# Attention and a normalised MLP on one core: the inverse deviation moved from GpSimd to two ScalarE activations, and the row made by one GpSimd instruction

## The chip, the cores and the metric

The kernel runs on one core of one Trainium2 chip. The metric is the device time of one execution in microseconds. The four executions of the kernel before lie between 312.97 and 314.12 us (0.4%), so differences of one percent are visible here. TensorE (PE) does the matrix products, VectorE (DVE) and ScalarE (ACT) do elementwise work and empty PSUM (the memory that matrix products are written to), GpSimd (POOL) casts and normalises rows, and SyncE (SP) issues transfers.

## The reference, cut to what matters

Eight batches of causal attention with a window of 64 (8 heads, 576 positions, head size 64) give rows `x` of 512 values. Each row is normalised and goes through a two-layer network with a residual:

```python
mu = np.mean(x, axis=-1, keepdims=True)
var = np.mean((x - mu) ** 2, axis=-1, keepdims=True)
xn = (x - mu) / np.sqrt(var + 1e-06) * g_ln
ch = np.maximum(xn @ w_ch1, 0.0) @ w_ch2
return x + ch
```

The change concerns `(x - mu) / sqrt(var + 1e-06)` alone. The kernel folds `g_ln` into the first weight matrix.

## The kernel before

The rows are handled in nine groups of 512 (the last holds the tails of all batches), and each group in four blocks of 128 rows. While TensorE runs the network of group g, the other engines prepare the rows of group g + 1. For groups 2 to 8 the row `z` of a block is made by four GpSimd instructions, from the mean and variance that VectorE left in `mvg`:

```python
def z_step(g, kb):
    z = p_blk.tile([128, DM], FP16, tag="z", ...)
    xv = x_norm[(g, kb // 2)][:, kb % 2, :]
    mu, var = mvg[g][:, kb, 0:1], mvg[g][:, kb, 1:2]
    # ... groups 0 and 1 go another way
    nc.gpsimd.tensor_scalar(out=ve, in0=var, scalar1=1.0, scalar2=EPS, op0=ALU.mult, op1=ALU.add)
    nc.gpsimd.tensor_tensor(out=rs, in0=ve, in1=mhalf, op=ALU.pow)
    nc.gpsimd.tensor_scalar(out=nm, in0=mu, scalar1=rs, scalar2=-1.0, op0=ALU.mult, op1=ALU.mult)
    nc.gpsimd.tensor_scalar(out=z, in0=xv, scalar1=rs, scalar2=nm, op0=ALU.mult, op1=ALU.add)
```

The first layer of a group is 16 units. Each fills one 128x512 PSUM tile with four matmuls, and ScalarE empties it with a Relu. There are only two such tiles (`bufs=2`), so TensorE can be at most two units ahead of ScalarE:

```python
ps_mm = ctx.enter_context(tc.tile_pool(name="psmm", bufs=2, space=PSUM))
def l1(hc):
    hps = ps_mm.tile([128, 512], FP32, tag="mm", ...)
    for kc in range(NKC):
        nc.tensor.matmul(out=hps, lhsT=w1g[:, kc, ...], rhs=zT[g][:, kc, :], ...)
    nc.scalar.activation(out=hrT[:, hc, :], in_=hps, func=AF.Relu, bias=0.0, scale=1.0)
```

The second layer is emptied by VectorE. Work for the next group is hung into numbered places after these units: `at(i, f, ...)` calls `f` after unit i. The built program keeps the written order for each engine, and the traces show ScalarE working through its instructions in that order, so a place decides what an instruction stands in front of.

The softmax here doesn't subtract the row's maximum and nothing guards it: scores larger than these inputs give would overflow.

Of the kernel before, what the change touches and what calls it, by code (L numbers as in the profile page):

```python
# [10 lines left out]
FP32 = mybir.dt.float32  # L11
# [3 lines left out]
AF = mybir.ActivationFunctionType  # L15
ALU = mybir.AluOpType
# [4 lines left out]
def kernel(  # L21
# [10 lines left out]
    nc = tc.nc  # L32
# [4 lines left out]
    NGRP = B + 1  # L37
# [3 lines left out]
    EPS = 1e-6  # L41
    XQ = 3
    XZ = 2
    scale = 1.0 / (D ** 0.5)
# [19 lines left out]
    mbias = p_const.tile([128, 64], FP16, tag="mbias", name="mbias")  # L64
    magt = p_const.tile([128, 4], FP32, tag="magt", name="magt")
    gT = p_const.tile([128, NKC], FP32, tag="gT", name="gT")
    mhalf = p_const.tile([128, 1], FP32, tag="mhalf", name="mhalf")
    w1g = p_const.tile([128, NKC, HID], FP16, tag="w1g", name="w1g")
    w2s = p_const.tile([128, NHC, DM], FP16, tag="w2s", name="w2s")
    w2v = w2s[:, :, :].rearrange("p (c e) (f d) -> p c e f d", e=2, f=2)  # L70
# [228 lines left out]
    def b_step(g, kb):  # L299
# [29 lines left out]
        if g < 2:  # L329
            z_step(g, kb)  # L330

    def z_step(g, kb):
        z = p_blk.tile([128, DM], FP16, tag="z", name=f"z_{g}_{kb}")
        zsd[(g, kb)] = z
        xv = x_norm[(g, kb // 2)][:, kb % 2, :]
        mu, var = mvg[g][:, kb, 0:1], mvg[g][:, kb, 1:2]
        if g < 2:
            nc.vector.tensor_scalar(out=z, in0=xv, scalar1=mu, scalar2=None, op0=ALU.subtract)
            return
        t = p_blk.tile([128, 3], FP32, tag="rsz", name=f"rsz_{g}_{kb}")  # L340
        ve, rs, nm = (t[:, i:i + 1] for i in range(3))
        nc.gpsimd.tensor_scalar(out=ve, in0=var, scalar1=1.0, scalar2=EPS, op0=ALU.mult, op1=ALU.add)  # L342
        nc.gpsimd.tensor_tensor(out=rs, in0=ve, in1=mhalf, op=ALU.pow)
        nc.gpsimd.tensor_scalar(out=nm, in0=mu, scalar1=rs, scalar2=-1.0, op0=ALU.mult, op1=ALU.mult)
        nc.gpsimd.tensor_scalar(out=z, in0=xv, scalar1=rs, scalar2=nm, op0=ALU.mult, op1=ALU.add)  # L345

    def zt_step(g, kb, eng="act"):
        z = zsd.pop((g, kb))
# [225 lines left out]
    nc.vector.memset(mask, 1.0)  # L574
    nc.vector.memset(magt, RSQRT_MAGIC)
    nc.vector.memset(ones1, 1.0)
    nc.vector.memset(mhalf, -0.5)
    nc.gpsimd.affine_select(
        out=mask[0:64], in_=mask[0:64], compare_op=ALU.is_gt, fill=0.0,
        base=0, channel_multiplier=1, pattern=[[-1, 64]],  # L580
# [85 lines left out]
    for g in range(NGRP):  # L666
        units, s_sums = mlp_units(g, (8, 16)[g] if g < 2 else 0, g == 0, g > 1)
        slots = [[] for _ in range(len(units) + 1)]

        def at(i, f, *a):  # L670
            slots[min(i, len(slots) - 1)].append((f, a))

        b = g + 1
        if g == 0:
            at(0, b_step, 0, 3)
            at(1, zt_step, 0, 2)
            at(3, zt_step, 0, 3)
            at(4, newton, 0, 0, 4)
            at(11, t_main, 1, 0, 0, 1)
            at(12, t_main, 1, 1, 0, 1)  # L680
            at(13, vB_cur, 1, 0, 1)
            at(13, vB_prev, 1, 0, 1)
            at(13, vB_cur, 1, 1, 1)
            at(13, vB_prev, 1, 1, 1)
            at(16, s_mm, 1, 0)
            at(16, s_mask, 1, 0)
            at(17, s_mm, 1, 1)
            at(17, s_mask, 1, 1)
            at(18, b_step, 1, 0)
            at(21, b_step, 1, 1)  # L690
            at(22, zt_step, 1, 0)
            at(24, zt_step, 1, 1)
            at(26, t_main, 1, 0, 1, 0)
            at(27, t_main, 1, 1, 1, 1)
            at(28, vB_cur, 1, 2, 0)
            at(28, vB_prev, 1, 2, 1)
            at(29, vB_cur, 1, 3, 0)
            at(29, s_mm, 1, 2)
            at(29, s_mask, 1, 2)
            at(30, s_mm, 1, 3)  # L700
            at(30, s_mask, 1, 3)
            at(30, load_v, 2, 0, 4)
            at(31, b_step, 1, 2)
        if g == 1:
            at(0, cast_qk, 2, 0)
            at(0, cast_qk, 2, 1)
            at(1, b_step, 1, 3)
            at(2, zt_step, 1, 2)
            at(13, newton, 1, 0, 4)
            at(5, zt_step, 1, 3)  # L710
            at(4, alloc_v, 2)
            at(4, alloc_qkT, 2)
            at(4, alloc_vB, 2)
            at(5, cast_v, 2, 0, 4)
            at(5, make_vB, 2)
            at(4, t_main, 2, 0, 0)
            at(4, t_main, 2, 1, 0)
            at(6, t_main, 2, 0, 1)
            at(6, t_main, 2, 1, 1)
            at(25, w2_sums, 3, 0, 4)  # L720
            at(28, w2_sums, 3, 4, 8)
            for j in range(4):
                at((9, 13, 16, 19)[j], s_mm, 2, j)
                at((10, 14, 17, 20)[j], s_mask, 2, j)
                at((13, 17, 20, 23)[j], b_step, 2, j)
                at((13, 17, 20, 23)[j], z_step, 2, j)
                at((18, 21, 24, 27)[j], zt_step, 2, j)
            at(3, load_qk, 3, 0)
            at(4, load_qk, 3, 1)
            at(7, load_v, 3, 0, 4)  # L730
            at(8, alloc_qkT, 3)
            at(8, cast_qk, 3, 0)
            at(10, cast_qk, 3, 1)
            at(14, alloc_v, 3)
            at(14, cast_v, 3, 0, 2)
            at(14, cast_v, 3, 2, 4)
            at(17, alloc_vB, 3)
            at(17, make_vB, 3)
            at(31, s_mm, 3, 0)
            at(31, s_mask, 3, 0)  # L740
            for i, (x, half) in zip((12, 24, 12, 28), ((0, 0), (1, 0), (0, 1), (1, 1))):
                at(i, t_main, 3, x, half, 0)
            at(40, load_qk, 4, 0)
            at(40, load_qk, 4, 1)
            at(40, load_v, 4, 0, 4)
        if g == 2:
            for m, i in enumerate((2, 1, 4)):
                at(4 + 2 * m, w2_sums, i, 0, 4)
                at(5 + 2 * m, w2_sums, i, 4, 8)
        if g > 1 and g + 2 < B:  # L750
            at(11, alloc_qkT, g + 2)
            if g + 2 >= XQ:
                at(11, cast_qk, g + 2, 0, (0,))
                at(11, cast_qk, g + 2, 1, (0,))
                at(11, cast_qk, g + 2, 0, (1,))
            else:
                at(11, cast_qk, g + 2, 0)
        if g > 1 and b < B:
            for j in range(4):
                if j:  # L760
                    at((2, 7, 12)[j - 1], s_mm, b, j)
                    at((3, 8, 13)[j - 1], s_mask, b, j)
                at((2, 7, 12, 17)[j], b_step, b, j)
                at((2, 7, 12, 17)[j], z_step, b, j)
                at((12, 12, 18, 23 if b in (3, 5) else 22)[j], zt_step, b, j)
        for n, i in enumerate(TAILS.get(g, ())):
            ts = (10, 11, 14, 20) if n else (1, 2, 5, 11)
            at(ts[0], s_mm, NGRP - 1, i)
            at(ts[1], s_mask, NGRP - 1, i)
            at(ts[2], b_step, NGRP - 1, i)  # L770
            at(ts[2], z_step, NGRP - 1, i)
            at(ts[3], zt_step, NGRP - 1, i)
        n = g + 2
        if g > 1 and n < B:
            at(16, cast_qk, n, 1, (1,) if n >= XQ else (0, 1))
            at(20, alloc_v, n)
            at(20, cast_v, n, 0, 2)
            at(21, cast_v, n, 2, 4)
            at(21, alloc_vB, n)
            at(21, make_vB, n)  # L780
            for i, (x, half) in zip((13, 17, 13, 21) if n >= XQ else (17, 19, 21, 25),
                                    ((0, 0), (1, 0), (0, 1), (1, 1))):
                at(i, t_main, n, x, half, 0)
            at(27, s_mm, n, 0)
            at(28, s_mask, n, 0)
            if n + 1 < B:
                at(40, load_qk, n + 1, 0)
                at(40, load_qk, n + 1, 1)
                at(40, load_v, n + 1, 0, 4)
        if g > 1:  # L790
            for i in range(1, 5):
                at(7 + i, s_sums, 0, 4, i)
                at(13 + i // 3, s_sums, 4, 6, i)
                at((15, 15, 19, 21)[i - 1], s_sums, 6, 8, i)
        for n, i in enumerate(TAILS.get(g + 1, ())):
            if n == 0:
                at(1, load_tail, i)
                at(24 if i < 2 else 18, cast_tail, i)
                at(27 if i < 2 else 22, t_tail, i, 0)
                at(29 if i < 2 else 22, t_tail, i, 1)  # L800
            else:
                at(25, load_tail, i)
        if len(TAILS.get(g, ())) == 2:
            at(3, cast_tail, TAILS[g][1])
            at(7, t_tail, TAILS[g][1], 0)
            at(8, t_tail, TAILS[g][1], 1)
        for i, u in enumerate(units):
            if g > 1 and i == 20:
                tbank["shared"] = True
            u()  # L810
            for f, a in slots[i]:
                f(*a)
        for f, a in slots[len(units)]:
            f(*a)
# [28 lines left out]
```

## Time and profile before

| | before |
|---|---|
| time, median of 4 executions | 313.62 us |
| TensorE busy | 298.9 us (95%) |
| ScalarE busy | 153.4 us (49%) |
| GpSimd busy | 166.3 us (53%) |
| share of GpSimd in the chain that ended last | 2% |

The profile page of the kernel before: busy time by engine (share of the span, number of instructions), and the chain of work that ended last, by engine.

```profile
PE 298.9 (95%) x3041; PEld 194.1 (62%) x3041; DVE 205.2 (66%) x385; ACT 153.4 (49%) x258; POOL 166.3 (53%) x251
...
PE 74%; DMA 10%; DVE 7%; SPq 4%; POOL 2%; ACT 1%; issue 1%; POOLq 0%; ACTq 0%
```

TensorE is the limit. Three quarters of the chain that ended last are matrix work, and GpSimd hardly appears in it.

The groups of instructions of the kernel before, from the view by line. The columns are line, engine, operation, output and input, shape and count, then total busy time in us and the mean of one in ns, then idle time of the engine just before and what ended it.

```profile
L392 PE MATMUL hps<-zT,w1g 128*128 128x512 f16 x480 | 110.4, 379 | 0.0
...
L396 ACT ACTIVATE hrT<-hps 128x512 f16<-128x512 f32 x120 | 71.9, 599 | 50.7 <-PE hps L392 47.2 <-issue 3.4
...
L212 ACT ACT_TABLE_LOAD x1 | 1.3, 1283 | 1.3 <-PEq L827 1.3
...
L345 POOL TENSOR_SCALAR z<-xn,rsz 128x512 f16<-128x512 f32 x28 | 25.3, 902 | 2.9
L343 POOL TENSOR_TENSOR rsz<-rsz,mhalf 128x1 f32<-128x1 f32 x28 | 19.3, 689 | 2.3
L344 POOL TENSOR_SCALAR rsz<-mvg,rsz 128x1 f32<-128x1 f32 x28 | 13.4, 480 | 2.8
L342 POOL TENSOR_SCALAR rsz<-mvg 128x1 f32<-128x1 f32 x28 | 10.7, 382 | 60.4 <-DVE mvg L328 59.8
```

TensorE never waits before a first-layer matmul (0.0). ScalarE has one table load in the whole run. The row itself takes 902 ns on GpSimd, and the three small instructions 382, 689 and 480 ns.

ScalarE's timeline of the kernel before, around the place where the change will put a pair (start and duration in us, then the idle time before and what ended it):

```profile
165.46 0.60 ACT L396 ACTIVATE hrT<-hps 128x512 f16<-128x512 f32 x1 [0.26 <-PE hps L392]
166.32 0.60 ACT L396 ACTIVATE hrT<-hps 128x512 f16<-128x512 f32 x1 [0.27 <-PE hps L392]
167.18 0.60 ACT L396 ACTIVATE hrT<-hps 128x512 f16<-128x512 f32 x1 [0.27 <-PE hps L392]
168.04 0.60 ACT L396 ACTIVATE hrT<-hps 128x512 f16<-128x512 f32 x1 [0.27 <-PE hps L392]
```

Each emptying takes 0.60 us and they follow each other every 0.86 us, so ScalarE has 0.27 us to spare per unit and no more.

### The profile page before, as it was taken

To read this page: it belongs to the slowest core of one execution; us is meant where nothing else is said; L and a number is where in the kernel's file an instruction comes from. 1 tells how busy PE (TensorE), PEld (TensorE's weight loads), DVE (VectorE), ACT (ScalarE), POOL (GpSimd) and SP (SyncE) were. 2 spreads that over 40 slices of the span, in tenths; PEclk is the share of its full clock that TensorE was granted. 3 is DMA by queue.
4 is the path that set the end of the run, shared out by engine and by line. 5 is a ranking of instruction groups with operands and counts; after the bars stand their busy time and mean duration, and the time that the engine had idled before them with its cause. 6 is when DMAs were issued, how large, how long until landed. Compare 5 with 4: busy or idle time off the path is not lost.

```text
span 313.0 us, 7473 instructions
## 1 busy us (share of the span) xinstructions
PE 298.9 (95%) x3041; PEld 194.1 (62%) x3041; DVE 205.2 (66%) x385; ACT 153.4 (49%) x258; POOL 166.3 (53%) x251
## 2 busy tenths in 40 slices
PE   6988998899999999999999999999999999999992
PEld 4457544497554468646964686459646855784582
DVE  1689585855674996589666965896669636751642
ACT  1496633477416752776247526762475058306500
POOL 7578666454760798369814983698145506200000
PEclk9999999999999999999999999999999999999999
DMA  8999999998866996798179997993690393003013
GB/s 192 267 390 290 320 336 272 280 304 184 159 144 196 268 206 105 243 312 147 37 212 316 203 149 219 316 142 67 209 172 19 62 209 117 2 2 134 0 36 101
DMA packets 109892, 57.42 MB, mean 183 GB/s; under 512 B 79841, under 2 KB 100833, under 8 KB 109858
## 3 DMA queue, kind: packets, MB, share of 16 engines
q1 hardware_dynamic: 108944, 54.02, 69.1%
q0 software_dynamic: 768, 2.80, 3.7%
q8 instruction: 24, 0.39, 0.5%
q10 hardware_dynamic: 146, 0.13, 0.1%
q14 instruction: 10, 0.08, 0.1%
HBM read 38.80 MB, written 9.44 MB: 154 GB/s over the span
## 4 chain that ended last, share of the span: by engine, by line
PE 74%; DMA 10%; DVE 7%; SPq 4%; POOL 2%; ACT 1%; issue 1%; POOLq 0%; ACTq 0%
PE hps L392 30%; PE pA L464 11%; PE pC L464 7%; PE pB L464 7%; PE ch L404 6%; DMA w2s<-in_moe_w_ch_dram 4%; DMA qk<-in_k_dram 4%; PE xps L317 3%; PE sc L283 3%; PE hph L513 3%; PE tp L226 2%; SPq L141 2%; DVE sS L443 2%; DMA w1s<-in_moe_w_ch_dram 2%; SPq L89 1%; DVE pt L297 1%
## 5 line engine op out<-in xcount | busy, mean ns | idle before, releaser
L392 PE MATMUL hps<-zT,w1g 128*128 128x512 f16 x480 | 110.4, 379 | 0.0
L396 ACT ACTIVATE hrT<-hps 128x512 f16<-128x512 f32 x120 | 71.9, 599 | 50.7 <-PE hps L392 47.2
L392 PEld LDWEIGHTS <-w1g 128*128 128x128 f16 x480 | 44.6, 98 | 49.3 <-issue 1.0
L290 ACT ACTIVATE pt<-sc 128x512 f16<-128x512 f32 x72 | 39.0, 595 | 29.8 <-DVE xn L471 15.6
L464 PEld LDWEIGHTS <-sS 128*128 128x128 f16 x448 | 43.3, 98 | 5.1
L342 POOL TENSOR_SCALAR rsz<-mvg 128x1 f32<-128x1 f32 x28 | 10.7, 382 | 60.4 <-DVE mvg L328 59.8
L128 POOL CAST qk<-qk 128x1024 f16<-128x1024 f32 x32 | 35.1, 1112 | 13.4 <-DMA qk<-in_q_dram 6.9
L464 PEld LDWEIGHTS <-hrT 128*128 128x128 f16 x336 | 32.6, 98 | 5.2
L212 ACT COPY qkT<-tp 128x1024 f16<-128x1024 f16 x16 | 16.1, 1012 | 35.2 <-PE tp L226 26.1
L297 DVE TENSOR_TENSOR pt<-pt,mask 128x1024 f16<-128x1024 f16 x32 | 25.4, 800 | 11.9 <-ACT pt L290 11.9
L471 DVE TENSOR_TENSOR xn<-pA,xn 128x512 f32<-128x512 f32 x28 | 19.2, 686 | 21.1 <-PE pA L464 21.1
L443 DVE TENSOR_TENSOR sS<-hrT 128x512 f16<-128x512 f16 (+1 forms) x42 | 24.8, 591 | 10.2 <-ACT hrT L396 10.2
L464 PE MATMUL pA<-wT,sS 128*128 128x256 f16 x224 | 26.9, 273 | 0.0
L345 POOL TENSOR_SCALAR z<-xn,rsz 128x512 f16<-128x512 f32 x28 | 25.3, 902 | 2.9
L464 PE MATMUL pC<-w2s,sS 128*128 128x256 f16 x224 | 26.8, 273 | 0.0
L325 DVE BATCH_NORM_STATS2 stats<-xn 128x6 f32<-128x512 f32 x36 | 25.0, 695 | 1.2
L323 DVE TENSOR_TENSOR xn<-xps,rcp 128x512 f32<-128x512 f32 x36 | 24.9, 692 | 1.2
L513 PE MATMUL hph<-zT,w1g 128*128 128x256 f16 x192 | 23.2, 272 | 2.3 <-ACT zT L360 1.1
L320 DVE RECIPROCAL rcp<-xps 128x8 f32<-128x8 f32 x36 | 7.4, 205 | 26.8 <-PE xps L317 26.8
L404 PE MATMUL ch<-w2s,hrT 128*128 128x512 f16 x96 | 23.1, 380 | 0.0
L513 PEld LDWEIGHTS <-w1g 128*128 128x128 f16 x192 | 18.3, 98 | 5.1 <-issue 2.6
L317 PEld LDWEIGHTS <-pt 128*64 128x64 f16 x576 | 12.2, 110 | 14.4 <-issue 6.4
(85 smaller groups left out, 395.1 us busy)
## 6 DMA issues: line engine op xcount, KB each, us to landing
out_dram<-xn SPq DMA_DIRECT2D x34, 256.0 KB, 2.6
qk<-in_q_dram SPq DMA_DIRECT2D x16, 512.0 KB, 6.2
qk<-in_k_dram SPq DMA_DIRECT2D x16, 512.0 KB, 7.4
v<-in_v_dram SPq DMA_DIRECT2D x32, 256.0 KB, 6.5
w2s<-in_moe_w_ch_dram SPq DMA_DIRECT2D x12, 512.0 KB, 5.7
w1s<-in_moe_w_ch_dram SPq DMA_DIRECT2D x4, 512.0 KB, 6.7
tk<-in_k_dram SPq DMA_DIRECT2D x8, 256.0 KB, 4.7
tv<-in_v_dram SPq DMA_DIRECT2D x8, 256.0 KB, 5.3
```

The costliest lines, as they stand in the source:

```text
L128: nc.gpsimd.tensor_copy(out=dst[:, :].rearrange("p (a j) e d -> p a e j d", j=j), in_=t[:, :].rearrange("p (a e j d) -> p a e j d", e=2, j ...
L290: nc.scalar.activation(out=o, in_=i, func=AF.Exp, bias=0.0, scale=scale)
L297: nc.vector.tensor_tensor(out=ptv, in0=ptv, in1=mb, op=ALU.mult)
L323: nc.vector.tensor_tensor(out=xn, in0=xps[:, :, 0:D], in1=rcp_b, op=ALU.mult)
L325: nc.vector.bn_stats(out=stats, in_=xv)
L345: nc.gpsimd.tensor_scalar(out=z, in0=xv, scalar1=rs, scalar2=nm, op0=ALU.mult, op1=ALU.add)
L392: nc.tensor.matmul(out=hps, lhsT=w1g[:, kc, 128 * hc:128 * (hc + 1)], rhs=zT[g][:, kc, :], start=(kc == 0), stop=(kc == NKC - 1),)
L396: nc.scalar.activation(out=hrT[:, hc, :], in_=hps, func=AF.Relu, bias=0.0, scale=1.0)
L404: nc.tensor.matmul(out=ch[kb], lhsT=hrT[:, hc, 128 * kb:128 * (kb + 1)], rhs=w2s[:, hc, :], start=(hc == 0), stop=(hc == NHC - 1),)
L443: nc.vector.tensor_tensor(out=o, in0=x, in1=y, op=op)
L464: nc.tensor.matmul(out=bank[which][:, p, :], lhsT=a[:, c, 128 * p:128 * p + 128], rhs=wv[:, c, :], start=(first and p == 0 and c == 0), st ...
L513: nc.tensor.matmul(out=hps[:, e], lhsT=w1g[:, kc, 128 * hc:128 * (hc + 1)], rhs=zT[g][:, kc, 256 * half:256 * half + 256], start=(kc == 0) ...
```

## The change

The intent is to free GpSimd: `(var + eps)^-0.5` becomes `exp(-0.5 * ln(var + eps))` in two one-column activations on ScalarE, which is only half busy, and the row becomes a single GpSimd instruction. Since the pair now stands in ScalarE's order, it is moved later (two units in group 2, three elsewhere), so that the variance is ready when ScalarE comes to it. In what follows the pair is one Ln and one Exp, and the scale of a row is the inverse deviation `rs` that they make.

```diff
-        t = p_blk.tile([128, 3], FP32, tag="rsz", name=f"rsz_{g}_{kb}")
-        ve, rs, nm = (t[:, i:i + 1] for i in range(3))
-        nc.gpsimd.tensor_scalar(out=ve, in0=var, scalar1=1.0, scalar2=EPS, op0=ALU.mult, op1=ALU.add)
-        nc.gpsimd.tensor_tensor(out=rs, in0=ve, in1=mhalf, op=ALU.pow)
-        nc.gpsimd.tensor_scalar(out=nm, in0=mu, scalar1=rs, scalar2=-1.0, op0=ALU.mult, op1=ALU.mult)
-        nc.gpsimd.tensor_scalar(out=z, in0=xv, scalar1=rs, scalar2=nm, op0=ALU.mult, op1=ALU.add)
+        t = p_blk.tile([128, 2], FP32, tag="rsz", name=f"rsz_{g}_{kb}")
+        lv, rs = t[:, 0:1], t[:, 1:2]
+        nc.scalar.activation(out=lv, in_=var, func=AF.Ln, bias=epst[:, 0:1], scale=1.0)
+        nc.scalar.activation(out=rs, in_=lv, func=AF.Exp, bias=0.0, scale=-0.5)
+        nc.gpsimd.tensor_scalar(out=z, in0=xv, scalar1=mu, scalar2=rs, op0=ALU.subtract, op1=ALU.mult)
@@ (group 2: two transposes' copies also go to ScalarE)
-            at(4, t_main, 2, 1, 0)
+            at(4, t_main, 2, 1, 0, 0)
-            at(6, t_main, 2, 1, 1)
+            at(6, t_main, 2, 1, 1, 0)
-                at((13, 17, 20, 23)[j], z_step, 2, j)
+                at((15, 19, 22, 25)[j], z_step, 2, j)
@@ (groups 3 to 7, then the tails)
-                at((2, 7, 12, 17)[j], z_step, b, j)
+                at((5, 10, 15, 20)[j], z_step, b, j)
-            at(ts[2], z_step, NGRP - 1, i)
+            at(ts[2] + 3, z_step, NGRP - 1, i)
```

The diff shows no table load, but the built program has them. A table load (`ACT_TABLE_LOAD` in the traces) is an instruction on ScalarE that the build puts before a function whose table set is not the one in place. This is ScalarE's order around one pair, as read from the built program:

```
L395 Activation hrT<-hps_5
L342 LoadActFuncSet
L342 Activation rsz<-mvg,epst      (Ln)
L343 LoadActFuncSet
L343 Activation rsz<-rsz           (Exp)
L395 Activation hrT<-hps_6
```

There are 57 loads in all, against one before: one in front of every Ln, and one in front of every following Exp.

## The prediction

> **What bounds it now.** TensorE. The page's first part gives PE 298.9 of 313.0 us (95%); GpSimd has 166.3 (53%) and ScalarE 153.4 (49%). The chain that ended last is 74% PE and only 2% GpSimd. From 96 us on, the windows view shows PE busy for nearly all of each stretch.
>
> **What it removes.** Three of four GpSimd instructions per block, 28 blocks: 382 + 689 + 480 ns (groups of lines 342 to 344), 43 us of GpSimd time. Nearly all is off the chain: I credit 1 us.
>
> **What it adds.** The built order of the changed kernel has 57 table loads on ScalarE against 1: one before each Ln and one before each following Exp, so the two functions are taken from different table sets. The trace before has one load, 1283 ns. The Trainium skill, "ScalarE: Activation LUTs", section "What ACT_TABLE_LOAD costs", agrees on 1283 ns, but adds about 1380 ns of drain to each switch; "ScalarE activation tables: per-element evaluation and per-set limits", section "What a function is on this engine", gives the load alone. The trace before, with one load at an idle start, cannot decide. I take the load alone (85%), the drain running beside it. The two one-column activations I put at 0.2 to 0.3 us each (estimate from the first page's 186 to 280 ns fixed cost). A pair then holds ScalarE for about 3.4 us; 28 pairs add some 85 us, so ScalarE's busy time goes from 153 to about 240 us (estimate).
>
> **How much lies on the chain.** In groups from the third on, ScalarE empties each 128x512 first-layer PSUM tile (599 ns) while TensorE fills the next (about 865 ns, read from the timeline, 0.27 us of ScalarE idle between). There are only two such buffers. The new places of the pair are after first-layer units 5 and 10 of each such group, and 8 for three tail blocks. TensorE fills both buffers and stops. Replaying by hand the two-buffer recurrence with those durations, two pairs in a group cost 5.2 us, three cost 7.7, one cost 3.1. Groups 2 to 6 with tails at 3 and 5: 3 x 5.2 + 2 x 7.7; group 7: 3.1; sum 34 us. The pairs after units 15 and 20 meet the second layer, emptied by VectorE, so they cost little: about 2 us each where TensorE itself transposes the row of block 3 (two groups), 1 at the last tail, 3 at the end of group 1, and 1 to 3 for later rows and copies. Sum about 43 us.
>
> **Prediction: 356 us, range 344 to 382.** Faster by over 2%: 0.02; within 2%: 0.03; slower: 0.95.
>
> **What shows each step right.** 57 loads near 1.28 us each and ScalarE busy near 240 us; GpSimd busy near 123 us; the waits view showing TensorE's first-layer matmuls waiting for ScalarE's emptying of line 395, two or three stops per group of 2 to 3 us, the chain of waits gaining tens of us of ScalarE; nothing of it in the first 75 us. Wrong: if each switch takes 2.7 us, a pair holds ScalarE 5.9 us, the same recurrence gives about 68 us for the first layers, and the time is near 400. If loads are hidden or dropped, it stays near 313.
>
> **What else would spoil it.** Stops long enough that TensorE's granted clock falls (then higher); GpSimd, waiting in order for each row's scale, delaying the casts behind it, and with them the transposes (higher); VectorE waits in group 2 absorbing part of the stop (lower).

## The result

| | before | after |
|---|---|---|
| time, median of 4 executions | 313.62 us | 368.10 us |
| lowest to highest | 312.97 to 314.12 | 367.79 to 368.47 |
| TensorE busy | 298.9 us | 313.5 us |
| mean granted TensorE clock | 0.999 | 0.968 |
| ScalarE busy | 153.4 us | 235.8 us |
| GpSimd busy | 166.3 us | 157.4 us |

The ratio is 1.174 (95% interval 1.171 to 1.177). A ratio here is the mean time of one kernel's fast runs over that of the other's of the same rounds, so it is not quite the ratio of the medians quoted. Executions in which one die ran at a lower clock are left out of the means.

The profile page of the changed kernel, the same two parts:

```profile
PE 313.5 (86%) x3041; PEld 197.2 (54%) x3041; DVE 205.1 (56%) x383; ACT 235.8 (64%) x372; POOL 157.4 (43%) x167
...
PE 32%; ACT 19%; DMA 13%; issue 11%; DVE 11%; POOL 8%; SPq 4%; POOLq 1%; ACTq 0%; DVEq 0%
```

TensorE's share of the chain fell from 74% to 32%, ScalarE's rose from 1% to 19% and GpSimd's from 2% to 8%.

The groups of the changed kernel that answer to those shown of before (lines 391 and 395 were 392 and 396):

```profile
L391 PE MATMUL hps<-zT,w1g 128*128 128x512 f16 x480 | 117.3, 393 | 23.4 <-ACT hrT L395 19.6 <-DMA zT<-z 3.3
...
L395 ACT ACTIVATE hrT<-hps 128x512 f16<-128x512 f32 x120 | 70.5, 597 | 45.0 <-PE hps L391 44.8
...
L342 ACT ACT_TABLE_LOAD x28 | 35.9, 1283 | 8.3 <-DVE mvg L328 7.9
L343 ACT ACT_TABLE_LOAD x28 | 35.9, 1283 | 0.5
...
L342 ACT ACTIVATE rsz<-mvg,epst 128x1 f32<-128x1 f32 x28 | 8.2, 295 | 0.3
...
L343 ACT ACTIVATE rsz<-rsz 128x1 f32<-128x1 f32 x28 | 5.7, 203 | 0.3
...
L344 POOL TENSOR_SCALAR z<-xn,mvg,rsz 128x512 f16<-128x512 f32 x28 | 59.1, 2110 | 124.5 <-ACT rsz L343 73.1 <-DVE stats L325 28.2 <-DMA tv<-in_v_dram 10.9
```

Two things stand out. The 56 new loads take 71.8 us of ScalarE, five times as much as the 13.9 us of the activations that need them. And the one remaining GpSimd instruction takes 2110 ns where the old one took 902 ns, so that GpSimd was relieved by 8.9 us instead of 43.

ScalarE's timeline of the changed kernel at one pair, in the first layer of group 4, at the same place as shown before:

```profile
186.97 0.60 ACT L395 ACTIVATE hrT<-hps 128x512 f16<-128x512 f32 x1 [0.27 <-PE hps L391]
187.58 1.28 ACT L342 ACT_TABLE_LOAD   x1
188.88 0.29 ACT L342 ACTIVATE rsz<-mvg,epst 128x1 f32<-128x1 f32 x1
189.19 1.28 ACT L343 ACT_TABLE_LOAD   x1
190.48 0.20 ACT L343 ACTIVATE rsz<-rsz 128x1 f32<-128x1 f32 x1
190.59 1.06 ACT L395 ACTIVATE hrT<-hps 128x512 f16<-128x512 f32 x2
```

The load ends at 187.58 + 1.28 = 188.86, and the Ln starts at 188.88. Each load costs its 1.28 us and nothing after it. From 187.58 to 190.59 the pair holds ScalarE for 3.0 us, during which no PSUM tile is emptied.

What TensorE waited for in the changed kernel (total in us, times, longest), longest first:

```profile
PE hps L391 <- ACT hrT L395: 19.6, 11, 2.6
PE ztp L356 <- POOL z L344: 7.5, 4, 2.3
PE hps L391 <- DMA zT<-z: 3.3, 2, 2.6
PE tp L226 <- POOL qk L128: 3.1, 6, 0.9
```

The first line is the stop that was forecast: 11 times, up to 2.6 us, TensorE waits for ScalarE to empty a first-layer tile. The same view of before has no such line. The second line is TensorE waiting for a GpSimd row that it has to transpose, and the fourth for a cast; that a late row on GpSimd held the cast up was not traced.

Busy time of each engine around the same pair of the changed kernel, by stretches of the span (columns: PE, PEld, DVE, ACT, POOL, granted clock, share of the DMA engines, GB/s):

```profile
188.50:191.20 2.70, 0.87 (x33) 0.72 (x33) 1.77 (x4) 2.66 (x6) 0.41 (x1) 1.00 0.97 315
191.20:192.20 1.00, 0.98 (x5) 0.49 (x5) 0.00 (x0) 1.00 (x3) 1.00 (x1) 0.96 1.08 372
192.20:195.60 3.40, 3.40 (x10) 1.20 (x8) 2.90 (x5) 1.51 (x3) 0.66 (x1) 0.51 1.07 247
195.60:197.50 1.90, 1.90 (x20) 0.78 (x18) 0.28 (x1) 1.79 (x2) 0.00 (x0) 1.00 0.99 226
```

During the stop TensorE is busy for 0.87 of 2.7 us. One microsecond after it resumes, it is granted half its clock for about 3.4 us, and its mean over the whole run is 0.968. The half clock follows some of the stops, not all. The kept traces show which. Every change of clock that they record lies a whole number of 3.41 us steps after the first one of its trace. Cut into stretches on that grid, the 13 traces at full speed hold 21 half-clock stretches before the last matmul (6 here, 15 in the four other runs below whose pairs with loads stop TensorE, none in the other eight), each 3.41 us long. Before each of the 21, TensorE was busy for 46% or less of the stretch (here 1.57 of the 3.42 us from 188.70 to 192.12). Of the 1163 other stretches only two were as idle (42% and 46%). So a stop is followed by the half clock where enough of it falls into one such stretch. That is how these traces go together; no run varies it alone.

### The profile page after: what moved, and what is told of

Same layout as the page of the kernel before. It is cut to its first block, busy times and chain, and to the rows that moved or that the text cites. A ratio compares the mean times of both kernels' runs of the same rounds, so it can differ in the third digit from the quotient of the medians.

```text
span 366.1 us, 7518 instructions
## 1 busy us (share of the span) xinstructions
PE 313.5 (86%) x3041; PEld 197.2 (54%) x3041; DVE 205.1 (56%) x383; ACT 235.8 (64%) x372; POOL 157.4 (43%) x167
## 4 chain that ended last, share of the span: by engine, by line
PE 32%; ACT 19%; DMA 13%; issue 11%; DVE 11%; POOL 8%; SPq 4%; POOLq 1%; ACTq 0%; DVEq 0%
PE hps L391 15%; ACT L342 6%; POOL z L344 5%; ACT L343 4%; PE pA L463 4%; DMA w2s<-in_moe_w_ch_dram 4%; DVE sS L442 4%; DMA qk<-in_q_dram 3%; ACT hrT L395 3%; PE pC L463 3%; ACT pt L290 3%; PE hph L512 3%; PE pB L463 3%; SPq L141 2%; DMA out_dram<-xn 2%
## 5 line engine op out<-in xcount | busy, mean ns | idle before, releaser
L391 PE MATMUL hps<-zT,w1g 128*128 128x512 f16 x480 | 117.3, 393 | 23.4 <-ACT hrT L395 19.6
L344 POOL TENSOR_SCALAR z<-xn,mvg,rsz 128x512 f16<-128x512 f32 x28 | 59.1, 2110 | 124.5 <-ACT rsz L343 73.1
L395 ACT ACTIVATE hrT<-hps 128x512 f16<-128x512 f32 x120 | 70.5, 597 | 45.0 <-PE hps L391 44.8
L391 PEld LDWEIGHTS <-w1g 128*128 128x128 f16 x480 | 46.4, 100 | 77.3 <-issue 31.7
L290 ACT ACTIVATE pt<-sc 128x512 f16<-128x512 f32 x72 | 39.0, 598 | 24.7 <-PE sc L283 24.4
L463 PEld LDWEIGHTS <-sS 128*128 128x128 f16 x448 | 44.5, 101 | 6.3
L342 ACT ACT_TABLE_LOAD x28 | 35.9, 1283 | 8.3 <-DVE mvg L328 7.9
L343 ACT ACT_TABLE_LOAD x28 | 35.9, 1283 | 0.5
L442 DVE TENSOR_TENSOR sS<-hrT 128x512 f16<-128x512 f16 (+1 forms) x42 | 27.7, 659 | 10.2 <-ACT hrT L395 10.2
L463 PE MATMUL pA<-wT,sS 128*128 128x256 f16 x224 | 28.3, 281 | 0.0
L463 PE MATMUL pC<-w2s,sS 128*128 128x256 f16 x224 | 28.1, 281 | 0.0
L212 ACT COPY qkT<-tp 128x1024 f16<-128x1024 f16 x18 | 17.8, 1011 | 6.4 <-PE tp L226 6.4
L512 PEld LDWEIGHTS <-w1g 128*128 128x128 f16 x192 | 18.3, 98 | 5.6 <-issue 3.1
```

The costliest lines, as they stand in the source:

```text
L290: nc.scalar.activation(out=o, in_=i, func=AF.Exp, bias=0.0, scale=scale)
L342: nc.scalar.activation(out=lv, in_=var, func=AF.Ln, bias=epst[:, 0:1], scale=1.0)
L343: nc.scalar.activation(out=rs, in_=lv, func=AF.Exp, bias=0.0, scale=-0.5)
L344: nc.gpsimd.tensor_scalar(out=z, in0=xv, scalar1=mu, scalar2=rs, op0=ALU.subtract, op1=ALU.mult)
L391: nc.tensor.matmul(out=hps, lhsT=w1g[:, kc, 128 * hc:128 * (hc + 1)], rhs=zT[g][:, kc, :], start=(kc == 0), stop=(kc == NKC - 1),)
L442: nc.vector.tensor_tensor(out=o, in0=x, in1=y, op=op)
```

## The experiments

Theory L: the loads, because of where they stand, stop TensorE, which then also loses clock. Rival Z: the long GpSimd row makes everything behind it late. Rival P: the rows' later places in the order do it. Every kernel below gave a correct result, and each ratio is against the kernel before on the same chip in the same rounds. "Over before" is the ratio less one, times 313.5 us.

### One table set for both functions

```diff
+    nc.scalar.preload_act_table_set("natural_log_exp_and_others")
     load_qk(0, 0)
```

The Trainium skill, "ScalarE: Activation LUTs", section "Table sets: the hidden batching unit", lists a set that has both functions. With it loaded at the start, the build placed no other load.

> The changed kernel with one table set loaded at the start that holds both Ln and Exp (and Copy and Relu), so that no switch is left: 1 table load in place of 57. Theory L (the loads, standing in ScalarE's order between the emptyings of the first layer, stop TensorE): ScalarE busy falls from 236 to about 164 us, the time to 313 to 326 us, the granted clock back to about 1.00. Rival Z (the new GpSimd row, 2.07 us where it was 0.80, makes rows, casts and transposes late): it stays above 340 us. Rival P (the rows' later places in the order): it stays well above 326 too.

Measured: 321.62 us as the median of the three fast executions (322.18 with the slow one), ratio 1.0267 (1.0232 to 1.0301). Its profiled execution fell into a slow state (435 us at clock 0.66), and the run was repeated for its profile:

> The run with one table set once more, since its profile fell into a slow state; wanted is a profile at full clock. L: 320 to 324 us as before, ScalarE busy about 164 us, TensorE's first layer waiting for ScalarE near 0; what is left over the kernel before (some 9 us) should show as TensorE waiting for GpSimd's rows (the 2.07 us form) or for what stands behind them, not for ScalarE.

Measured: 322.50 us, ratio 1.0266, ScalarE busy 165.6 us, clock 0.995. The profile's ScalarE and GpSimd groups of the repeat:

```profile
L343 ACT ACTIVATE rsz<-rsz 128x1 f32<-128x1 f32 x28 | 5.7, 203 | 0.9
...
L563 ACT ACT_TABLE_LOAD x1 | 1.3, 1283 | 0.8 <-PEq L827 0.8
...
L344 POOL TENSOR_SCALAR z<-xn,mvg,rsz 128x512 f16<-128x512 f32 x28 | 67.9, 2425 | 71.8 <-ACT rsz L343 56.9 <-DMA tv<-in_v_dram 8.8 <-DVE sS L442 6.1
```

TensorE's waits for the first layer's emptying are gone from its list, and 46 of the 54.5 us came back. The loads are the larger part. But the row is still long without them (2425 ns), so the loads are not what made it long, and 8.3 us are left over before. Of the wait for GpSimd's rows that was expected in their place, the trace shows 4.2 us (5 times).

### The loads kept, the row as before

```diff
+        nc.gpsimd.tensor_scalar(out=nm, in0=mu, scalar1=rs, scalar2=-1.0, op0=ALU.mult, op1=ALU.mult)
-        nc.gpsimd.tensor_scalar(out=z, in0=xv, scalar1=mu, scalar2=rs, op0=ALU.subtract, op1=ALU.mult)
+        nc.gpsimd.tensor_scalar(out=z, in0=xv, scalar1=rs, scalar2=nm, op0=ALU.mult, op1=ALU.add)
```

> The changed kernel with its 57 loads, but the row made by multiply-and-add with a negated mean as before (two GpSimd instructions a block). L: 355 to 368 us, so at most some 13 us gained, as the loads remain. Z: 314 to 335 us. If the row's form matters it falls from about 2.07 to about 0.8 us on GpSimd; if the length came from contention with other engines, it stays near 2 us.

Measured: 352.60 us, ratio 1.1267 (1.1200 to 1.1333), a little below the 355 to 368 us that theory L had given, and far above the 314 to 335 us of rival Z. The row's group in it:

```profile
L345 POOL TENSOR_SCALAR z<-xn,rsz 128x512 f16<-128x512 f32 x28 | 21.5, 766 | 2.9
```

The row fell to 766 ns. So the long row cost the changed kernel 54.5 - 39.7 = 14.8 us. Rival Z as the main cause is out, but it is a real part.

### Both

The single set and the multiply-and-add row together.

> Both of the above: one table load, row by multiply-and-add. L with a small Z: 310 to 318 us, within 2% of the kernel before, since GpSimd was never what bounds; the difference to the run with one set alone is the price of the slow row without loads, 0 to 10 us. P: above 320 us, since the late places stay.

Measured: 318.05 us, ratio 1.0137 (1.0101 to 1.0172). It came out just above the 310 to 318 us expected. Without the loads the long row costs only 8.3 - 4.3 = 4 us. With them it costs 14.8 us. That the scale then comes late and the long row adds to the delay is the likely reason, argued and not shown.

### Four forms of the row, in the kernel before

```diff
+        if kb == 0:    # nm = -mu*rs
+            nc.gpsimd.tensor_scalar(out=z, in0=xv, scalar1=rs, scalar2=nm, op0=ALU.mult, op1=ALU.add)
+        elif kb == 1:
+            nc.gpsimd.tensor_scalar(out=z, in0=xv, scalar1=mu, scalar2=rs, op0=ALU.subtract, op1=ALU.mult)
+        elif kb == 2:  # nm = mu*rs
+            nc.gpsimd.tensor_scalar(out=z, in0=xv, scalar1=rs, scalar2=nm, op0=ALU.mult, op1=ALU.subtract)
+        else:          # nm = -mu
+            nc.gpsimd.tensor_scalar(out=z, in0=xv, scalar1=nm, scalar2=rs, op0=ALU.add, op1=ALU.mult)
```

> The kernel before (no Ln, no loads, old places), but with the GpSimd row in four forms by block: block 0 multiply then add, block 1 subtract then multiply (the changed kernel's form), block 2 multiply then subtract, block 3 add then multiply; all give the same values. If the form sets the time: block 0 about 0.8 us, block 1 about 2.07 us; blocks 2 and 3 tell whether it is the subtraction (2 slow, 3 fast) or the order of the two (2 fast, 3 slow). If the changed kernel's long rows came from its loads or from contention: all four near 0.8 us. Time 312 to 318 us.

Measured: 321.79 us in its one execution, correct; 312 to 318 us had been expected. The row's instructions by form, from the view of the tile `z` (duration in ns, least/median/most; lines 346, 348, 351 and 354 are blocks 0 to 3):

```profile
L346 POOL TENSOR_SCALAR z<-xn,rsz x7: 762/774/775, 80.9 to 236.0; 128x512 f16<-128x512 f32 x7
L348 POOL TENSOR_SCALAR z<-xn,mvg,rsz x7: 2082/3214/3690, 85.0 to 241.1; 128x512 f16<-128x512 f32 x7
L351 POOL TENSOR_SCALAR z<-xn,rsz x7: 2077/2142/2552, 90.1 to 269.5; 128x512 f16<-128x512 f32 x7
L354 POOL TENSOR_SCALAR z<-xn,rsz x7: 767/767/768, 94.3 to 278.5; 128x512 f16<-128x512 f32 x7
```

The two forms with a subtraction take at least 2.08 us, in either order, and the two with an addition 0.77 us. All four use two per-row scalars, and blocks 0 and 2 even the same tiles. It is the subtraction. Why block 1 took longer still (median 3214 ns against 2142 ns of block 2) was not pursued. Fourteen such rows alone took the kernel from about 313 to 321.8 us (one execution). That is more than the 4 us of 28 such rows with the single set, so the price of a long row seems to depend on what else GpSimd has to do (argued). Here it keeps the three small instructions (busy 182.0 us), and TensorE waits 4.5 us for its casts, against 0.3 us in the kernel before.

### The places alone

The kernel before with only the `at(...)` lines of the change.

> The kernel before with only the changed places: each block's four GpSimd instructions stand three units later, and the two transposes' evacuations on ScalarE as in the change. L and Z: 311 to 318 us, the rows have slack. P: 330 us or more.

Measured: 314.30 us, ratio 1.0021 (1.0005 to 1.0038). Rival P, the places by themselves, is out: 0.7 us.

### Pairs that nobody reads

The rows stay as before, on GpSimd. An Ln and an Exp are added on ScalarE at the changed places, into a tile of their own, and the two transposes' copies of group 2 go to ScalarE as in the change. One run has all 28 pairs, one the 13 inside a first layer, one the other 15.

```diff
+    def dummy(g, kb):
+        if not (...):          # all; or the 13; or the 15
+            return
+        t = p_blk.tile([128, 2], FP32, tag="dum", ...)
+        nc.scalar.activation(out=t[:, 0:1], in_=mvg[g][:, kb, 1:2], func=AF.Ln, bias=epst[:, 0:1], scale=1.0)
+        nc.scalar.activation(out=t[:, 1:2], in_=t[:, 0:1], func=AF.Exp, bias=0.0, scale=-0.5)
...
+                at((5, 10, 15, 20)[j], dummy, b, j)
```

> The kernel before, its rows untouched, with an Ln and an Exp added on ScalarE at the changed places, whose results nobody reads: 57 loads, but no row waits for them and the row is the fast one. L: 345 to 362 us (the first layers' stops alone, 34 us, plus some copies). Z: 313 to 320 us, since without the slow row in the chain nothing is late.

> As the run with all the unread pairs, but only the 13 that stand inside a first layer (blocks 0 and 1 of groups 3 to 7, and the tails at unit 8): 27 loads. L: 13 stops of about 2.6 us, so +30 to +36 us over the kernel before, 343 to 350 us. If a stop of 3.0 us of ScalarE costs TensorE less than the two-buffer recurrence says: below 338 us.

> As the run with all the unread pairs, but only the 15 others (group 2, blocks 2 and 3 of groups 3 to 7, last tail): 31 loads. L: small, +1 to +9 us, 314 to 322 us, since VectorE empties the second layer. If every pair costs alike: +30 us or more.

| unread pairs | loads | time | ratio | over before |
|---|---|---|---|---|
| all 28 | 57 | 347.77 us | 1.1086 | 34.0 us |
| 13 in a first layer | 27 | 346.30 us | 1.1055 | 33.1 us |
| the other 15 | 31 | 315.38 us | 1.0067 | 2.1 us |

This is the clearest result. Equal pairs cost 2.5 us each in a first layer and 0.14 us each elsewhere. Of the run with 13 pairs, the busy times of its page:

```profile
PE 307.5 (89%) x3041; PEld 196.8 (57%) x3041; DVE 208.8 (60%) x384; ACT 190.8 (55%) x312; POOL 162.1 (47%) x251
```

And the view of TensorE's waits of the same run, two lines:

```profile
PE hps L400 <- ACT hrT L404: 22.2, 14, 2.6
PE sc L284 <- ACT tkT L213: 2.5, 1, 2.5
```

The 33.1 us come in two parts of different kinds: 22.2 + 2.5 us in which TensorE waits for ScalarE, and 307.5 - 298.9 = 8.6 us in which the same 3041 matmuls take longer, at a mean clock of 0.976. The trace has four half-clock stretches of 3.41 us, filled with matmuls, which make up about 4 x 1.7 = 6.8 of these 8.6 us; the rest was not followed.

### Loads kept, but moved out of the first layer

In groups 3 to 7 the pairs of blocks 0 to 2 become one Ln and one Exp of three columns after unit 15, and the tails' pairs move to places after units 16 and 17. The row is made by adding a negated mean, then multiplying.

```diff
-                at((5, 10, 15, 20)[j], z_step, b, j)
-                at((12, 12, 18, 23 if b in (3, 5) else 22)[j], zt_step, b, j)
+                if j == 2:
+                    at(15, rs_step, b, 0, 3)     # Ln and Exp of three columns
+                    for jj in range(3):
+                        at(15, z_step, b, jj)    # the rows
+                elif j == 3:
+                    at(20, rs_step, b, 3, 4)
+                    at(20, z_step, b, 3)
+                at((17, 17, 18, 23 if b in (3, 5) else 22)[j], zt_step, b, j)
@@ (tails)
-            at(ts[2] + 3, z_step, NGRP - 1, i)
-            at(ts[3], zt_step, NGRP - 1, i)
+            at(16 if n == 0 else 17, rs_step, NGRP - 1, i, i + 1)
+            at(16 if n == 0 else 17, z_step, NGRP - 1, i)
+            at(19 if n == 0 else 20, zt_step, NGRP - 1, i)
```

> The loads kept (37 in place of 57), but moved: in groups 3 to 7 one Ln and one Exp for blocks 0 to 2 together after unit 15, the tails' pairs after unit 16 or 17, so that no pair stands inside a first layer; row by add then multiply with a negated mean made ahead (no subtraction). L (a load costs only where it stands between two emptyings of the first layer): 314 to 322 us, although 36 loads are left. If a load costs wherever it stands: 36 of 56 of the 34 us, so 333 us or more.

Measured: 340.15 us, ratio 1.085 (1.079 to 1.091). I had expected 314 to 322 us, so this is a miss. TensorE's longest waits in it:

```profile
PE ztp L364 <- POOL z L342: 10.5, 4, 3.7
PE tp L226 <- POOL qk L128: 4.1, 2, 2.0
```

The first layer no longer waits for ScalarE at all. But I had left too little room behind the pairs: TensorE's transposes of rows follow only three units later, and waited for rows that were not ready. The longest of these waits, 3.7 us, is for a tail's row in group 3, whose scale had to wait for two pairs on ScalarE (6.2 us), its own being the second. The clock fell as well (0.979), with TensorE's busy time up from 298.9 to 306.3 us. So a load costs where something behind it is soon wanted: the next emptying in one kernel, the row in this one. These waits and the clock account for some 22 of the 26.6 us, and the rest was not pursued.

### Two tries to win back the last percent

Both have the single set and a row by add then multiply (negated mean made ahead of the scale). One has pairs and rows one unit earlier. The other leaves them at the change's places and moves two of TensorE's row transposes two units later.

> One table set, row by add then multiply with the negated mean made before the scale comes, pairs and rows one unit earlier than in the change for groups 3 to 8. If what one set with the fast row still loses (318 against 313.3 us) is the row coming late after the scale: 312.5 to 316 us. If it is the 56 short activations on ScalarE themselves: it stays at 317 to 319 us. Not expected to beat the kernel before, since TensorE is busy there for nearly all of the time from 96 us on.

> One table set, pairs and rows at the change's places (not earlier), row by add then multiply with the negated mean made ahead, and the TensorE transposes of block 3's row in the two groups that do them on TensorE two units later. If what one set with a fast row still lost (318 against 313.4 us) is TensorE waiting for those two rows (3.3 us of waits in that profile): 313 to 315.5 us, with TensorE's waits for GpSimd's row near 0. If it stays at 317 to 319: the short activations on ScalarE, or something else, cost it.

Measured: 317.71 us (ratio 1.0134) and 317.85 us (ratio 1.0127), so neither moved, where 312.5 to 316 and 313 to 315.5 us had been given for a late row as the cause. In the second, TensorE's waits for GpSimd's rows vanished from the list, as hoped, but this line took their place:

```profile
PE pA L464 <- DVE xn L471: 3.7, 4, 1.6
```

The first has 2.6 us of this line and no wait for rows either. The wait moved from one engine to another with no gain. What holds the last 4 us over before was not settled. A pair without loads still takes 0.29 + 0.20 us of ScalarE in a stage with 0.27 us to spare per unit, but no run took that away alone. No version beat the kernel before, whose TensorE is busy nearly throughout.

## Why the prediction was right or wrong

The time, 368.1 us, lies in the range of 344 to 382 us, 12 us above the 356 us predicted.

- **"57 table loads on ScalarE against 1", 1283 ns each, without a drain behind them.** Right: 57 loads, 1283 ns each, next activation 0.02 us after the load's end, and no more than 0.3 us of idle time in all before the 28 Lns. ScalarE's busy time was put at about 240 us and is 235.8 us.
- **"A pair then holds ScalarE for about 3.4 us".** A little too long: 3.0 us.
- **"two pairs in a group cost 5.2 us, three cost 7.7, one cost 3.1 ... sum 34 us".** The 13 pairs alone measured 33.1 us. The agreement is partly luck. With the true 3.0 us, 0.4 us less for each of the 13, the forecast would have been about 28.8 us (an estimate), and the waits measured 24.7 us. Most of the other 8.6 us is TensorE's half clock (about 6.8 us), which the prediction named only as something that could spoil it.
- **The other pairs and later rows cost about 9 us in all.** This is the term that was mis-sized. The 15 other pairs cost 2.1 us by themselves, but rows waiting for their scale, and the long row above all, brought the rest of the change to 54.5 - 33.1 = 21.4 us. By steps: the other pairs 34.0 - 33.1 = 0.9 (within the noise of the two runs), rows that wait for a scale 39.7 - 34.0 = 5.7, the long row 14.8. The split depends on the order of the steps, as the long row alone shows: 4 us without the loads.
- **"GpSimd busy near 123 us".** Wrong: 157.4 us. The prediction subtracted three small instructions and never asked what the fourth would cost in its new form. It took the old duration for an instruction with a different operation in it, and 28 x 1.2 us were missing.
- **Stops of 2 to 3 us, two or three a group, tens of us of ScalarE in the chain, nothing in the first 75 us.** The kind and place are right, the length is not: the waits view has 11 stops, 19.6 us in total, so 1.8 us on average, the longest 2.6. ScalarE is 19% of the chain, some 70 us. The first new load comes at 80.5 us. The first layer of group 2 starts at 100.8 instead of 96.5 us, 4.3 us where 3 had been given to the end of group 1; 2.6 of them are TensorE's wait for the DMA transpose of a late row.

## What to carry to other kernels

A half-busy engine is not free: ask how long its order can be held before the next instruction that someone waits for, here 0.27 us per unit with two PSUM tiles in between, and read the built program for instructions that the diff does not show, such as table loads. Load one table set that has every function you alternate between, before the first use. And when an instruction changes its operation, measure it again; its old duration does not carry over even with the same shape.

## What the Trainium skill lacked or had wrong

- "ScalarE: Activation LUTs", section "What ACT_TABLE_LOAD costs", puts a switch at about 2.66 us, load and drain. Here a load took 1283 ns, as it says, but the next activation started 0.02 us after it: a switch costs 1.3 us in a running stream, as "ScalarE activation tables: per-element evaluation and per-set limits" has it.
- The latter page, section "Table sets in the compiler and the runtime", says that the loads are placed per block, by greedy longest run. A set that serves both functions exists and was not chosen in this program: 56 loads for 28 pairs. Loading that set explicitly at the start left one. Whether the page's rule was applied to this program and came out so, or another was used, no run shows.
- "GPSIMD Engine Reference", section "3.1 Elementwise — side-by-side cycle accounting", gives 769 ns as a best case for 512 elements, which the rows with an addition match (767 to 774 ns). No page says that a subtraction in the same instruction takes 2.1 us or more.
- "TensorE: Matmul & The Clock Gate", Part 1, has the clock fall to half after an idle window of about 3.4 us. Here it fell to half after a stretch of 3.42 us in which TensorE was still busy for 1.57 us, and stayed so for 3.41 us. No page gives the share of busy time below which this happens; in these traces all 21 cases had 46% or less.
